# One core, state-space convolution beside windowed attention: where the next chunk's first sines stand in ScalarE's queue

## The chip, the cores and the metric

The kernel runs on one core of a Trainium2 chip. The metric is the device time of one execution in microseconds (us). The core has five engines with a queue each, in which instructions run in order: TensorE (PE in the profile), VectorE (DVE), ScalarE (ACT), GpSimd (POOL) and SyncE (SP). SyncE issues most of the transfers between the core's memory and DRAM. An engine that meets an instruction whose inputs are not there waits, and all that is queued behind the instruction waits with it.

## The reference

Two independent computations share the core; their outputs stand side by side. Part A is attention over a dilated window of 8 keys (32 heads of 20). Part B is a long convolution whose filter is a sum of 192 complex exponentials for each of 640 channels:

```python
P = jnp.exp(logdA[:, :, None] * l[None, None, :])       # (640, 192, 2048), complex
K = jnp.einsum("dn,dnl,dn->dl", Cc, P, dB).real         # the filter, 2048 long
Kf = rfft(pad(K)); Uf = rfft(pad(u))
y = irfft(Uf * Kf)[:2048] + u * Dskip
```

The output is `concatenate([attention, y])`, 2048 rows of 1280.

## The kernel before

Part B's 640 channels are worked in five chunks of 128 (`for c in range(NCH)`, L750). A position l is split into digits, so that each exponential is a product of small tables, and each chunk builds its filter in two halves (h = 0 and 1), each of two units.

- `coefficients` (L204) writes two more forms of the chunk's coefficients `cT`, and `exps_chunk` (L215) the real exponentials `R` for the whole chunk, 45 ScalarE instructions at L224. `R` has two buffers, for even and odd chunks.
- `trig_half` (L228) makes one half's sines and cosines. TensorE forms the phases in PSUM (L249, L253), and ScalarE takes the sine at L261: four instructions into `TA`, then four into `TX`. `TA` has a buffer for each half, `TX` one in all, so the next half's `TX` is written when the X products of this half have read it.
- `small_half` (L272) multiplies `R`, `cT`, `TA` and `TX` on VectorE (helper line L278, and L293) into F, G and X. Its first instruction, "P<-R,TA" in the trace, opens the half.
- Each unit makes three Y on VectorE (`y_form`, L312, four buffers), multiplies them with X on TensorE (`kgen_unit`, L327), and ScalarE copies the result into `Ksb` (L328), the chunk's filter.

The filter of chunk c is transformed in chunk c + 1. In `fwd` (L331) TensorE works in two steps (L341, L347), and ScalarE copies after each (`A` at L342, `Sg` at L348). In `products` (L352) SyncE loads the transform of the input twice from DRAM, into P1 (L358) and, with its halves exchanged, into P2 (L359, L360), and VectorE multiplies each with the filter's transform (L362). P2 lies where the first step's copy `A` lay, so its load waits until TensorE has read `A` in L347. `inverse_a` (L368) needs both products: TensorE at L378, ScalarE's copies `Z` at L379. Then comes the transform of the input for the next chunk but one (`fwd_u`, L395), with the same two steps and copies.

In a chunk above 0 the calls stand in this order: the first half's small products; the transform of the last chunk's filter; the second half's sines; unit 0; the two products and `inverse_a`; unit 1; `fwd_u`; the second half's small products; then the lines that the change touches; then units 2 and 3. After the last chunk's inverse comes attention: projection of the keys (`proj_k`, L477, and `k_halo`, L486), the chunk's last units (L327), projection of the queries (L495).

The order on an engine is not the order of the calls: a scheduler places instructions by when it takes their inputs to be ready. `issue_after(x)` queues what its block records on x's engine behind x; `keep_in_program_order` queues an instruction behind all recorded before it. PSUM has three two-bank buffers, shared by the phases, both steps of `fwd` and `inverse_a`.

Switching ScalarE between sines and exponentials takes an instruction of its own, ACT_TABLE_LOAD in the trace, put ahead of the first of the other kind.

Of the kernel before, what the change touches and what calls it, by code (L numbers as in the profile page):

```python
# [203 lines left out]
def coefficients(engine, B, c):  # L204

    co = B["cT"][:, c]
    if engine.engine == mybir.EngineType.Activation:
        engine.activation(out=co[:, :, 1], in_=co[:, :, 2], func=ACT.Copy, scale=-1.0)
        engine.copy(out=co[:, :, 3], in_=co[:, :, 0])
    else:  # L210
        engine.tensor_scalar(out=co[:, :, 1], in0=co[:, :, 2], scalar1=-1.0, scalar2=None, op0=A.mult)
        engine.tensor_copy(out=co[:, :, 3], in_=co[:, :, 0])


def exps_chunk(tc, pools, B, c):  # L215
    nc = tc.nc
    R = pools["tab"].tile([128, 48, NE_R, 4], bf16, name="R", tag=f"R{c % 2}")
    src = B["alpha"][:, c].rearrange("p u (q f) -> p (u q) f", f=4)
    nc.gpsimd.memset(R[:, :, 0:16:8, :], 1.0)
    nc.gpsimd.memset(R[:, :, 47, :], 1.0)  # L220
    for e, m in enumerate(R_MULT):
        if m == 0.0:
            continue
        last = nc.scalar.activation(out=R[:, :, e, :], in_=src, func=ACT.Exp, scale=m)  # L224
    return R, last
# [463 lines left out]
def body(tc, ctx, pools, prm, B_u, B_Dskip, Sd, Zd, UDd, A_x, A_wqkv, A_wo, out_a, out_b):  # L689
# [13 lines left out]
    R, trig = {}, {}  # L703
    with tc.tile_pool(name="prep_b", bufs=1) as pb, tc.tile_pool(name="prep_c", bufs=1) as pc, tc.tile_pool(name="prep_a", bufs=1) as pa, tc.tile_pool(name="psum_p", bufs=2, space=bass.MemoryType.PSUM) as psp:
        pools.update(prep_a=pa, prep_b=pb, prep_c=pc)
        B, fill = partB_prep(tc, dict(pools, psum=psp), prm)
# [43 lines left out]
    for c in range(NCH):  # L750
# [32 lines left out]
        with ExitStack() as order:  # L783
            if c > 0:
                order.enter_context(tc.issue_after(last.ins))
            F, G, Xs = small_half(tc, pools, B["cT"][:, c], R[c], *trig[c, 1][:2], 1)
        if c < LAST:
            if c > 0:
                with tc.issue_after(trig[c, 1][2].ins):
                    coefficients(nc.scalar, B, c + 1)  # L790
                    R[c + 1] = exps_chunk(tc, pools, B, c + 1)[0]
            trig[c + 1, 0] = trig_half(tc, pools, B, c + 1, 0)
        else:
            att.open_q0()
        with ExitStack() as order:
# [70 lines left out]
    for i0, ni, j0, nj, done in ((0, 128, 2, 3, 0), (128, 128, 2, 3, 1), (256, 128, 0, 4, None), (256, 256, 4, 1, 2), (384, 128, 0, 4, 3)):  # L866
        if done == 1:
            att.sums(1)
        for w in range(W):
# [4 lines left out]
            if (done, w) in LOADS:  # L874
                qr, c = LOADS[done, w]
# [12 lines left out]
def kernel(  # L888
# [28 lines left out]
    Zd = dpool.tile([NCH, 128, 4096], bf16, name="Zdram")  # L917
    UDd = dpool.tile([NCH, 128, 2048], bf16, name="UDdram")
    body(tc, ctx, pools, prm, B_u, B_Dskip, Sd, Zd, UDd, A_x, A_wqkv, A_wo, out_a, out_b)


# [28 lines left out]
```

## Time and profile before

| | us |
|---|---|
| median of 3 runs | 425.13 |
| lowest, highest | 423.94, 426.79 |
| the profiled execution | 420.77 |
| its span, first to last instruction | 419.0 |

The prediction quotes the profile's page and answers of the trace. A timeline row has the start (us from the span's start), the time from the first start to the last end in the row, the engine, the line, the operation, its output and input with their sizes, how many instructions the row merges, and in brackets the idle time before it and what ended that. Neighbouring instructions of one engine overlap a little, so the pace in a queue is read from start to start. A row of the chain of waits has start, length, engine or DMA, line or tile. The chunks of the loop can be told from the rows "P<-R,TA" on VectorE: chunk 2 begins with the one at 129.74, its second half at 156.80, chunk 3 at 180.62 and 207.65, chunk 4 at 230.27 and 259.49.

### The profile page before, as it was taken

The page shows a single profiled execution, that of the slowest core. Times are in us where ns is not written, and L with a number is a line of the kernel's source. Part 1 is how long each engine was busy: PE and PEld are TensorE (multiplying, and loading weights), DVE is VectorE, ACT ScalarE, POOL GpSimd, SP SyncE. Part 2 cuts the span into 40 slices and gives each one's busy share as a digit, 9 for nine tenths or more (in the row PEclk, how much of TensorE's full clock was granted, in tenths as well). Part 3 has the DMA queues.
Part 4 walks back from the last instruction along what each step waited for, and adds up shares of the span by engine and source line. Part 5 has one row for each costly group of instructions (what it writes and reads, how often), then busy time and mean ns, then how long its engine had stood idle before and what let it go on. Part 6 is the DMA issues. An engine that isn't in the chain of part 4 may idle for free.

```text
span 419.0 us, 17105 instructions
## 1 busy us (share of the span) xinstructions
PE 341.1 (81%) x7757; PEld 227.0 (54%) x7757; DVE 382.7 (91%) x381; ACT 310.5 (74%) x571; POOL 47.9 (11%) x85
## 2 busy tenths in 40 slices
PE   2375678989886887778868688999899999799996
PEld 1133463866864567455754557455555676444444
DVE  7999999999997999999999988994986899899762
ACT  3989996889999899979999492533667645754752
POOL 7540000000000000000000000170000300502110
PEclk9997598999899899989999899999999999969999
DMA  5599002164233403334029990440040292897544
GB/s 144 171 228 171 3 2 96 60 231 102 103 129 127 102 5 127 129 128 102 28 104 295 185 256 9 157 167 2 3 102 0 85 207 81 221 237 214 156 127 127
DMA packets 45129, 51.57 MB, mean 123 GB/s; under 512 B 31376, under 2 KB 38992, under 8 KB 42368
## 3 DMA queue, kind: packets, MB, share of 16 engines
q1 hardware_dynamic: 41520, 41.40, 36.7%
q0 software_dynamic: 3392, 8.95, 7.2%
q8 instruction: 61, 1.00, 1.0%
q10 hardware_dynamic: 144, 0.12, 0.1%
q14 instruction: 12, 0.10, 0.1%
HBM read 28.01 MB, written 18.35 MB: 111 GB/s over the span
## 4 chain that ended last, share of the span: by engine, by line
PE 33%; DVE 23%; ACT 19%; DMA 11%; issue 7%; SPq 6%; DVEq 0%; ACTq 0%
DVE Y L312 9%; DMA P<-Sdram 5%; ACT A L342 5%; ACT R L224 5%; PE ps_k L327 4%; PE ps_q L495 4%; PE ps_k L477 4%; PE ps_v L508 4%; PE ps_op L426 4%; DVE X L278 3%; ACT Sg L348 3%; PE ps_o L426 2%; DMA U<-in_B_u_dram 2%; DVE P L362 2%; PE ps_l L548 2%
## 5 line engine op out<-in xcount | busy, mean ns | idle before, releaser
L312 DVE TENSOR_TENSOR Y<-F,G 128x3072 bf16<-128x3072 bf16 x60 | 102.9, 1757 | 0.0
L327 PE MATMUL ps_k<-Y,X 64*32 64x64 bf16 (+1 forms) x3840 | 81.5, 237 | 20.5 <-DVE Y L312 14.5
L327 PEld LDWEIGHTS <-X 64*32 64x32 bf16 (+1 forms) x3840 | 62.2, 115 | 46.7 <-issue 32.8
L224 ACT ACTIVATE R<-LPC 128x192 bf16<-128x192 f32 x225 | 59.6, 358 | 0.1
L249 PE MATMUL ps_ph<-LPC 128*128 128x512 bf16 x100 | 32.2, 424 | 13.2 <-DMA LPC<-lo 6.2
L348 ACT CAST Sg<-ps_f 128x1024 bf16<-128x1024 f32 x40 | 37.7, 1025 | 6.1 <-PE ps_f L347 6.0
L342 ACT CAST A<-ps_f 128x1024 bf16<-128x1024 f32 x40 | 38.0, 1040 | 2.1 <-PE ps_f L341 2.0
L347 PE MATMUL ps_f<-A,T 128*128 128x128 bf16 x320 | 23.8, 235 | 16.0 <-ACT A L342 14.2
L278 DVE TENSOR_TENSOR X<-R,TX 128x1536 bf16<-128x1536 bf16 x40 | 36.5, 958 | 0.0
L261 ACT ACTIVATE TA<-ps_ph 128x1024 bf16<-128x1024 int16 (+1 forms) x40 | 30.4, 828 | 6.1 <-PE ps_ph L249 3.6
L606 DVE TENSOR_TENSOR prod<-v,atp 128x2048 bf16<-128x2048 bf16 (+2 forms) x32 | 30.8, 1018 | 2.4 <-PE ps_o L426 1.5
L347 PEld LDWEIGHTS <-T 128*128 128x128 bf16 x320 | 21.7, 106 | 17.8 <-issue 16.7
L261 ACT ACTIVATE TX<-ps_ph 128x1024 bf16<-128x1024 int16 (+1 forms) x40 | 29.6, 839 | 1.1 <-PE ps_ph L253 1.1
L537 DVE TENSOR_TENSOR prod<-qT,kT 128x1024 bf16<-128x1024 bf16 (+1 forms) x16 | 23.0, 1483 | 4.7 <-ACT qT L496 4.7
L362 DVE TENSOR_TENSOR P<-P,Sg 128x4096 bf16<-128x4096 bf16 x10 | 22.8, 2290 | 4.6 <-DMA P<-Sdram 2.6
L426 PE MATMUL ps_op<-wo,o 128*128 128x320 bf16 x160 | 26.3, 301 | 0.1
L638 ACT CAST ob<-ps_op 128x320 bf16<-128x320 f32 x28 | 12.0, 429 | 16.9 <-PE ps_op L426 15.6
L378 PE MATMUL ps_ia<-EA,P 128*128 128x128 bf16 x320 | 21.5, 220 | 2.9 <-DVE P L362 2.8
L328 ACT CAST Ksb<-ps_k 128x512 bf16<-128x512 f32 x20 | 11.7, 601 | 16.1 <-PE ps_k L327 16.0
L495 PE MATMUL ps_q<-xT,wkq 128*128 128x512 bf16 x100 | 22.6, 379 | 0.0
L477 PE MATMUL ps_k<-xT,wkq 128*128 128x512 bf16 x100 | 22.4, 379 | 0.0
L379 ACT CAST Z<-ps_ia 128x1024 bf16<-128x1024 f32 x20 | 19.4, 1014 | 3.7 <-PE ps_ia L378 3.7
(133 smaller groups left out, 601.7 us busy)
## 6 DMA issues: line engine op xcount, KB each, us to landing
Sdram<-Sg SPq DMA_DIRECT2D x5, 1024.0 KB
P<-Sdram SPq DMA_DIRECT2D x5, 1024.0 KB
P<-Sdram SPq DMA_DIRECT2D x10, 512.0 KB
Zdram<-Z SPq DMA_DIRECT2D x5, 1024.0 KB
Z<-Zdram SPq DMA_DIRECT2D x30, 128.0 KB
U<-in_B_u_dram SPq DMA_DIRECT2D x4, 640.0 KB
UDdram<-UD SPq DMA_DIRECT2D x10, 256.0 KB
out_dram<-ysb SPq DMA_DIRECT2D x32, 80.0 KB
```

Source lines behind the costliest of these rows:

```text
L224: last = nc.scalar.activation(out=R[:, :, e, :], in_=src, func=ACT.Exp, scale=m)
L249: MM(full[:, 16 * gi:16 * gi + 16], lhsT=L[b][:, 0:128], rhs=C, start=(i == 0), stop=(i == len(ops) - 1))
L261: last = nc.scalar.activation(out=dst[:, q0:q0 + nq, 0:32, :].rearrange("p q e f -> p e q f"), in_=words.rearrange("p (e q f) -> p e q f", ...
L278: TT = lambda o, a, b, op: V.tensor_tensor(out=o, in0=a, in1=b, op=op)
L312: nc.vector.tensor_tensor(out=Y[:].rearrange("p q (b a) f -> p q b a f", a=8), in0=fa, in1=gb, op=A.mult)
L327: MM(ps[32 * g:32 * g + 32, t], lhsT=X[hb, q, 2 - k, :, f], rhs=Ys[k][hb, q, :, f], start=(t == 0 and n == 0), stop=(n == 5), tile_positio ...
L342: nc.scalar.copy(out=A1[:, :, 32 * b:32 * b + 32].rearrange("p k (j g) -> p k j g", g=4), in_=ps[:].rearrange("p j k g -> p k j g"))
L347: last = MM(ps[:, kk], lhsT=C["T2"][:, 8 * b + kk, :], rhs=A1[:, 8 * b + kk, :], start=(kk % 4 == 0), stop=True, skip_group_check=True)
L348: nc.scalar.copy(out=Sg[:, :, 8 * b:8 * b + 8, :], in_=ps[:].rearrange("p k (j g) -> p j k g", g=4))
L426: self.MM = lambda *a, **k: late(self.nc.tensor.matmul(*a, **k))
L477: MM(ps[:, i], lhsT=self.wk[:, kt, 128 * ct:128 * ct + 128], rhs=self.x4[:, kt, 2 * i:2 * i + 2, 256 * hf:256 * hf + 256], start=(kt == 0) ...
L495: MM(ps[:, i], lhsT=self.wq[:, kt, 128 * ct:128 * ct + 128], rhs=self.x4[:, kt, 2 * i:2 * i + 2, 256 * hf:256 * hf + 256], start=(kt == 0) ...
```

## The change

The call that makes the sines of the next chunk's first half is moved ahead of the block with the coefficient forms and the exponentials, and the block is queued on ScalarE behind these sines (`trig_half` returns `TA`, `TX` and its last sine) instead of behind those of the current chunk's second half. This applies to c = 1, 2 and 3. In chunk 0 the block stands elsewhere, and the last chunk has no next one.

```diff
         if c < LAST:
+            trig[c + 1, 0] = trig_half(tc, pools, B, c + 1, 0)
             if c > 0:
-                with tc.issue_after(trig[c, 1][2].ins):
+                with tc.issue_after(trig[c + 1, 0][2].ins):
                     coefficients(nc.scalar, B, c + 1)
                     R[c + 1] = exps_chunk(tc, pools, B, c + 1)[0]
-            trig[c + 1, 0] = trig_half(tc, pools, B, c + 1, 0)
```

The built programs hold the same number of instructions of each kind, 11 table loads among them, and the same order on SyncE and GpSimd. ScalarE's order from the sines of chunk 1's second half on is, before: Ksb, coefficient forms, table load, 7 exponentials, Ksb, 4 exponentials, Z three times, 1 exponential, Z, A four times, 3 exponentials, Sg four times, 30 exponentials, table load, 8 sines, Ksb twice, A of the next chunk. After: Ksb twice, Z, A and Sg four times each, 8 sines, coefficient forms, table load, 45 exponentials, Ksb twice, A of the next chunk four times, Sg four times, table load, 8 sines of that chunk's second half. At the two later places the Ksb and Z stand a little differently among each other, and the exponentials that stood between the copies before are more.

The scheduler moves other work with it. On VectorE, in the first half of chunks 2 to 4, the products with the first 16 of X's 32 exponent rows come for both units first, then a Y (in chunk 4 two), then those with the other 16; and five Y stand ahead of the first L362 product and one between the two, where before three stood ahead and the other three between or behind. In chunk 4 the negation of TX (L293) comes ahead of the half's first product, too. In chunks 2 and 3 a UD product (L391) comes ahead of the second L362 instead of behind. On TensorE a few tens of kgen_unit's multiplications (37 in chunk 2, 50 in chunk 3, 13 in chunk 4) stand between the two steps of the filter's transform. In chunk 4, 15 multiplications of the inverse, 34 of kgen_unit and 48 of the inverse follow the last phase, then proj_k's 50, then all 25 of k_halo (before, 21 of these stood ahead of the inverse).

## The prediction

> **What bounds it now.** I read the page's busy times first, then the busy time by stretches of the chunks, then the timelines of VectorE and ScalarE, and last the chain of waits where the loop ends.
>
> ```profile
> span 419.0 us, 17105 instructions
> PE 341.1 (81%) x7757; PEld 227.0 (54%) x7757; DVE 382.7 (91%) x381; ACT 310.5 (74%) x571; POOL 47.9 (11%) x85
> ```
>
> ```profile
> 156.00:180.00 24.00, 18.54 (x447) 13.81 (x439) 24.00 (x23) 23.09 (x46) 0.62 (x2) 0.95 0.28 112
> ...
> 230.00:259.00 29.00, 22.16 (x683) 16.95 (x681) 25.77 (x23) 16.78 (x22) 0.15 (x1) 0.94 0.82 164
> 259.00:300.00 41.00, 39.99 (x716) 23.00 (x705) 34.74 (x34) 17.51 (x21) 9.17 (x4) 1.00 0.23 84
> ```
>
> Columns three to six are PE, PEld, DVE, ACT after the stretch and its length. In the chunks VectorE is all but full (24.00 of 24.00) and ScalarE nearly so (23.09); behind 259 TensorE is the full one (39.99 of 41.00). So an edit on ScalarE can give at most VectorE's few idle spots, and what it gives counts only if TensorE's late stretch starts earlier. VectorE's timeline holds these spots and the marks that I use:
>
> ```profile
> 101.23 2.28 DVE L362 TENSOR_TENSOR P<-P,Sg 128x4096 bf16<-128x4096 bf16 x1
> ...
> 129.74 0.96 DVE L278 TENSOR_TENSOR P<-R,TA 128x1536 bf16<-128x1536 bf16 x1 [2.33 <-ACT TA L261]
> ...
> 135.89 2.69 DVE L278 TENSOR_TENSOR X<-R,TX 128x1536 bf16<-128x1536 bf16 x3
> ...
> 146.11 2.29 DVE L362 TENSOR_TENSOR P<-P,Sg 128x4096 bf16<-128x4096 bf16 x1
> 148.31 1.75 DVE L312 TENSOR_TENSOR Y<-F,G 128x3072 bf16<-128x3072 bf16 x1
> 149.98 2.29 DVE L362 TENSOR_TENSOR P<-P,Sg 128x4096 bf16<-128x4096 bf16 x1
> ...
> 155.52 1.36 DVE L391 TENSOR_TENSOR UD<-U,Dsb 128x1024 bf16<-128x1024 bf16 x1
> 156.80 0.95 DVE L278 TENSOR_TENSOR P<-R,TA 128x1536 bf16<-128x1536 bf16 x1
> ...
> 180.62 0.96 DVE L278 TENSOR_TENSOR P<-R,TA 128x1536 bf16<-128x1536 bf16 x1
> ...
> 207.65 0.97 DVE L278 TENSOR_TENSOR P<-R,TA 128x1536 bf16<-128x1536 bf16 x1
> ...
> 230.27 0.98 DVE L278 TENSOR_TENSOR P<-R,TA 128x1536 bf16<-128x1536 bf16 x1
> ...
> 248.74 2.29 DVE L362 TENSOR_TENSOR P<-P,Sg 128x4096 bf16<-128x4096 bf16 x1 [2.00 <-ACT TA L261]
> ...
> 253.94 2.29 DVE L362 TENSOR_TENSOR P<-P,Sg 128x4096 bf16<-128x4096 bf16 x1 [1.24 <-DMA P<-Sdram]
> ```
>
> There are three idle spots, and only the first, 2.33 us ahead of chunk 2, waits for the sines that the change moves. Chunks 3 and 4 start without a wait. In chunk 4 the waits of 2.00 and 1.24 are for loads (the sine named at 248.74 can't be it, since that product reads none).
>
> **ScalarE's queue, step by step.** These rows give the pace of each kind:
>
> ```profile
> 100.06 0.42 ACT L208 ACTIVATE cT<-cT 128x192 bf16<-128x192 bf16 x1
> ...
> 100.73 1.28 ACT L224 ACT_TABLE_LOAD   x1
> ...
> 114.05 3.76 ACT L348 CAST Sg<-ps_f 128x1024 bf16<-128x1024 f32 x4 [0.33 <-PE ps_f L347]
> 117.67 7.73 ACT L224 ACTIVATE R<-LPC 128x192 bf16<-128x192 f32 x30
> 125.42 1.28 ACT L261 ACT_TABLE_LOAD   x1
> 126.71 2.92 ACT L261 ACTIVATE TA<-ps_ph 128x1024 bf16<-128x1024 int16 x4
> ...
> 132.26 1.16 ACT L328 CAST Ksb<-ps_k 128x512 bf16<-128x512 f32 x2
> 133.20 3.88 ACT L342 CAST A<-ps_f 128x1024 bf16<-128x1024 f32 x4
> ```
>
> From start to start: coefficient forms 100.73 - 100.06 = 0.67, table load 126.71 - 125.42 = 1.29, one exponential (125.42 - 117.67) / 30 = 0.258, eight sines 132.26 - 126.71 = 5.55, two Ksb 0.94.
>
> Nothing is removed or added; the gain must come from order. Before, the chunk's first product needs two table loads, all 45 exponentials (15 of them slipped in between the copies) and four sines. After, it needs eight sines, the forms, one load and the 7 exponentials of the first eight rows; the others run beside VectorE. The price is that the slots among the copies, once used by 15 exponentials, the forms and a load (15 x 0.258 + 0.67 + 1.29 = 5.8 us), fall empty, because TensorE feeds the copies there no faster:
>
> ```profile
> 103.57 3.84 PE L378 MATMUL ps_ia<-EA,P 128*128 128x128 bf16 x61 [0.60 <-DVE P L362]
> 107.33 4.04 PE L341 MATMUL ps_f<-BD,U 128*64 128x128 bf16 x64
> 113.00 3.42 PE L347 MATMUL ps_f<-A,T 128*128 128x128 bf16 x32 [1.63 <-ACT A L342]
> ```
>
> The inverse starts as the second product ends (101.23 + 2.28 = 103.51), the next transform right behind it until 111.37, and the second step at 113.00. Sg ends at 117.81, 14.3 after the product. Without exponentials in between, the last copy of A could start some 0.5 us earlier, at 111.4; so Sg ends 13.8 after the product (bounds 13.3 and 14.3). From there: exponentials begin at 13.8 + 5.55 + 0.67 + 1.29 = 21.3 behind the second product; 7 are done at 23.1, 14 (for G) at 24.9, 30 (first X products) at 29.0, all 45 at 32.9.
>
> At one place a rule speaks against the new order. The row has the next activation 1.29 after the load starts. The Trainium skill, page "ScalarE: Activation LUTs", section "What ACT_TABLE_LOAD costs", puts a switch at about 1.28 us for the load and 1.38 for a drain. By that the load, which the new order keeps on the way to a chunk's first product, would hold each of the three starts up to 1.38 more, about 2.7 us in all after the margins found below, and the sum would come out some 1.2 us slower than before; the trace shows the 1.28 and no drain.
>
> **Chunk 2.** VectorE is free at 129.74 - 2.33 = 127.41, the seven exponentials are there at 103.51 + 23.1 = 126.6, G's at 128.4 against 128.3. P starts at about 127.5, 2.2 us earlier. The first X product comes 135.89 - 129.74 = 6.2 later, at 133.7, and the third, behind two X (2.69 / 3 = 0.9 each) and a Y (149.98 - 148.31 = 1.67), at 137.1; their rows are there at 132.5 and 136.4, so they don't wait.
>
> The exponentials that were early are now late for ScalarE's next work: they end at 136.4, so the copies A of the filter's transform start at 137.3 instead of 133.20, and the P2 load, which waits for them, moves with it. This takes the row of the load's issue and its flight from the chain of waits:
>
> ```profile
> 140.51 0.45 SPq L359 DMA_DIRECT2D P<-Sdram  x1
> ```
>
> ```profile
> 141.01 6.34 DMA P<-Sdram
> ```
>
> ```profile
> 191.56 6.45 DMA P<-Sdram
> ```
>
> ```profile
> 244.39 9.43 DMA P<-Sdram
> ```
>
> From A's start to the issue it was 140.51 - 133.20 = 7.3; so it is issued at 144.7 and has landed at 144.7 + 0.5 + 6.34 = 151.5. VectorE comes to the second product later than before, as two Y and a UD now stand ahead: 127.5 + (146.11 - 129.74) + 2 x 1.67 + (149.98 - 146.11) + 1.28 = 152.4. So the load is covered by 0.9 us. The product ends at 154.6, and, with those Y and UD done already, the second half starts there instead of at 156.80: 2.2 us are kept.
>
> **Chunks 3 and 4.** From the second half's start to the next chunk's P VectorE takes 180.62 - 156.80 = 23.8 against ScalarE's 23.1: no wait, P at 178.4. All 45 exponentials are there at 187.5, the load at 187.5 + 0.9 + 7.3 + 0.5 + 6.4 = 202.6, and VectorE comes to it 24.9 after P, at 203.3 (margin 0.7). The second half starts at 205.5 instead of 207.65. To chunk 4 it is 230.27 - 207.65 = 22.6 of VectorE with, in the new order, a TX negation (0.47) moved ahead of P, so P falls at 228.6, even with ScalarE. In chunk 4 the exponentials end at 238.4, A starts at 239.4, P2 is issued at 246.7 and lands at 253.6, later than VectorE's 251.7. Here the load ends last, as it did before at 253.94, and the gain shrinks. I take 6.45 for it: its 9.43 of before flew beside the P1 load, which waited behind the transposes of x:
>
> ```profile
> 225.82 16.42 SPq L436 DMA_TRANSPOSE xT<-in_A_x_dram  x4
> 242.34 0.52 SPq L358 DMA_DIRECT2D P<-Sdram  x1
> ```
>
> The transposes stand behind the store of a UD in SyncE's queue and start 2 us earlier with it, so P1 goes out at about 240.3, and it is done before P2 starts. The second product ends at 255.8.
>
> ```profile
> 255.10 0.69 PE L486 MATMUL ps_kh<-xT,wkq 128*128 128x42 bf16 x21
> ...
> 262.71 10.95 PE L477 MATMUL ps_k<-xT,wkq 128*128 128x512 bf16 x50
> ```
>
> Behind it TensorE has 63 multiplications of the inverse (3.84 by the row of 61 above) and 34 of a unit (0.8), with no Y left to wait for, where before it waited for two: proj_k starts at about 260.5 instead of 262.71, 2.2 earlier. Of these 0.7 go to the 21 multiplications of k_halo that filled a gap before and now stand behind proj_k. **Sum: 1.5 us earlier**, handed on whole through the stretch that TensorE fills. Against the profiled execution that is 420.8 - 1.5 = 419.3; that execution is 4.4 below the median of the three runs, and the same 1.5 off the median gives 423.6.
>
> **Rivals.** *The load is on time in chunk 4 too* (lands by 251.7): then proj_k starts 1.9 earlier still, 3.4 in all, 421.7. For it speaks that TensorE's second step in chunk 4 may run closer behind A than in chunk 2, against it the transposes beside it (the DMA share is 0.82 in 230 to 259).
>
> *The sines are held by TensorE.* The phases stand between a unit's multiplications in TensorE's queue, and one gap of this kind is in the trace:
>
> ```profile
> 177.56 0.60 ACT L261 ACTIVATE TA<-ps_ph 128x512 bf16<-128x512 int16 x1 [0.89 <-PE ps_ph L253]
> ...
> 180.93 0.60 ACT L261 ACTIVATE TX<-ps_ph 128x512 bf16<-128x512 int16 x1 [0.36 <-PE ps_ph L253]
> ```
>
> With 0.89 + 0.36 = 1.25 in each chunk, less the margins 0.8, 0.7 and 0, the three starts lose 2.3, and the end is 0.8 later than before, 425.9. Against it, the first chunk's and the later sines of the trace ran without a gap.
>
> *Slower: the P2 load takes the wait's place.* It is now issued 4 us later in each chunk and covered by only 0.9 and 0.7. If it takes 9.43 instead of 6.4, the second product waits 2.2, 2.3 and 3.0, and each wait delays the inverse, the copies, the sines and the exponentials behind it, so they add: 7.5 - 1.5 = 6.0 slower, 431.1. It decides from a flight of about 7.3 us on. Against it: both undisturbed flights took 6.4.
>
> That the change does nothing is excluded by the order of ScalarE's queue; that its effect is lost is the second rival.
>
> **Numbers.** Chances: my forecast 0.50, on time in chunk 4 0.15, held sines 0.20, late load 0.15. A measurement of this kernel can tell about 1% (4.3 us) from no change; its three runs alone spread over 2.9. My forecast's own range is 421.5 to 425.5. The whole range is from 421.7 less half that spread, 420.0, to past the held sines, 428.0; the late load's upper part is left out. Faster by over 1% only by the first rival with scatter, 0.10; slower the late load, 0.15; within 1% 0.75.
>
> **What would show it.** Right: no wait for a sine ahead of chunk 2's P, chunk 3's and 4's P at about 178 and 229, ScalarE empty for some 5 us among the copies, 45 exponentials in one run, and L477 starting 2 us earlier. Wrong: waits on "P<-R,TA" or G for R in chunks 3 and 4, a wait for P<-Sdram ahead of the second L362 in chunks 2 or 3, gaps between sines for ps_ph, or a late stretch of another length behind L477.

## The result, and the profile after

| | before | after |
|---|---|---|
| median of 6 runs, us | 424.53 | 428.71 |
| lowest to highest, us | 419.50 to 427.67 | 425.18 to 430.08 |
| the profiled execution, us | 420.77 | 429.62 |

The changed kernel takes 1.0125 of the time before, with a 95% interval of 1.0078 to 1.0171: some 1.2% slower. The forecast was 0.4% faster. Ratios here and below leave out executions more than 1.5% above the fastest of their kernel, and three of the profiles below are of such executions (the new order in chunks 1 and 2 alone, half of the units' multiplications in the old order, fewer exponentials in the new one).

The page of the changed kernel shows that the engines' busy times hardly grew, but for TensorE's (by 4.1 us, of which 4.0 lie in the run's last stretch, shown below; VectorE and ScalarE by 0.8 each):

```profile
span 427.8 us, 17099 instructions
PE 345.2 (81%) x7757; PEld 227.2 (53%) x7757; DVE 383.5 (90%) x381; ACT 311.3 (73%) x571; POOL 41.2 (10%) x85
```

So up to that last stretch waits are what is new. Among the page's groups, the Y on VectorE show it; the last field is the idle time ahead of them and what ended it. First the group before, then after:

```profile
L312 DVE TENSOR_TENSOR Y<-F,G 128x3072 bf16<-128x3072 bf16 x60 | 102.9, 1757 | 0.0
```

```profile
L312 DVE TENSOR_TENSOR Y<-F,G 128x3072 bf16<-128x3072 bf16 x60 | 103.4, 1764 | 4.9 <-PE ps_k L327 4.9
```

Before, no Y ever waited. Now VectorE, the engine that is all but full, waits 4.9 us for TensorE to read an earlier Y and free its buffer, 4.3 of them ahead of the projection of the keys (L477). VectorE's timeline after has the places:

```profile
103.10 0.99 DVE L278 TENSOR_TENSOR P<-R,TA 128x1536 bf16<-128x1536 bf16 x1
...
126.95 0.99 DVE L278 TENSOR_TENSOR P<-R,TA 128x1536 bf16<-128x1536 bf16 x1
128.46 0.96 DVE L278 TENSOR_TENSOR G<-R,TA 128x1536 bf16<-128x1536 bf16 x1 [0.52 <-ACT R L224]
...
154.63 0.96 DVE L278 TENSOR_TENSOR P<-R,TA 128x1536 bf16<-128x1536 bf16 x1
...
174.51 1.76 DVE L312 TENSOR_TENSOR Y<-F,G 128x3072 bf16<-128x3072 bf16 x1 [0.52 <-PE ps_k L327]
176.71 1.76 DVE L312 TENSOR_TENSOR Y<-F,G 128x3072 bf16<-128x3072 bf16 x1 [0.45 <-PE ps_k L327]
...
180.74 0.96 DVE L278 TENSOR_TENSOR P<-R,TA 128x1536 bf16<-128x1536 bf16 x1 [1.01 <-ACT R L224]
...
207.84 0.94 DVE L278 TENSOR_TENSOR P<-R,TA 128x1536 bf16<-128x1536 bf16 x1
...
231.44 0.96 DVE L278 TENSOR_TENSOR P<-R,TA 128x1536 bf16<-128x1536 bf16 x1 [0.46 <-ACT R L224]
...
252.61 1.76 DVE L312 TENSOR_TENSOR Y<-F,G 128x3072 bf16<-128x3072 bf16 x1 [3.31 <-PE ps_k L327]
...
258.15 2.28 DVE L362 TENSOR_TENSOR P<-P,Sg 128x4096 bf16<-128x4096 bf16 x1
```

The wait of 2.33 us for a sine ahead of chunk 2 is gone, and the second half of chunk 2 opens at 154.63 instead of 156.80. By chunk 3 (180.74 against 180.62) the lead is lost: two Y wait for TensorE, then the chunk's first product for its exponentials. In chunk 4 another Y waits 3.31 us.

TensorE's timeline after tells why it is late (a merged row's length runs from its first start to its last end):

```profile
136.81 1.07 PE L341 MATMUL ps_f<-BD,Ksb 128*64 128x128 bf16 x16 [6.43 <-ACT Ksb L328]
...
140.92 2.67 PE L347 MATMUL ps_f<-A,T 128*128 128x128 bf16 x24
...
153.98 2.30 PE L327 MATMUL ps_k<-Y,X 64*32 64x64 bf16 x122
156.80 0.88 PE L327 MATMUL ps_k<-Y,X 64*32 64x64 bf16 x38 [0.52 <-issue]
157.62 1.01 PE L378 MATMUL ps_ia<-EA,P 128*128 128x128 bf16 x15
...
257.55 2.83 PE L327 MATMUL ps_k<-Y,X 64*32 64x64 bf16 x150
261.70 0.29 PE L327 MATMUL ps_k<-Y,X 64*32 64x64 bf16 x8 [1.32 <-issue]
261.92 1.01 PE L378 MATMUL ps_ia<-EA,P 128*128 128x128 bf16 x15
...
266.33 10.96 PE L477 MATMUL ps_k<-xT,wkq 128*128 128x512 bf16 x50
...
281.22 2.12 PE L495 MATMUL ps_q<-xT,wkq 128*128 128x512 bf16 x9
```

In the middle of the filter's transform TensorE stands still for 6.43 us, until ScalarE copies Ksb (the same wait is 6.44 in chunk 3 and 3.42 in chunk 4). What it could not do then it does later, together with the multiplications of the second unit, and the inverse runs in earnest only from 157.62, 3.0 us behind the product that it was waiting for. ScalarE's timeline after shows the other side:

```profile
123.46 1.28 ACT L224 ACT_TABLE_LOAD   x1
124.76 11.53 ACT L224 ACTIVATE R<-LPC 128x192 bf16<-128x192 f32 x45
136.17 1.07 ACT L328 CAST Ksb<-ps_k 128x512 bf16<-128x512 f32 x2
137.11 3.75 ACT L342 CAST A<-ps_f 128x1024 bf16<-128x1024 f32 x4
...
154.09 0.60 ACT L261 ACTIVATE TX<-ps_ph 128x512 bf16<-128x512 int16 x1 [1.47 <-PE ps_ph L253]
...
158.71 1.01 ACT L379 CAST Z<-ps_ia 128x1024 bf16<-128x1024 f32 x1 [3.54 <-PE ps_ia L378]
...
167.32 3.76 ACT L348 CAST Sg<-ps_f 128x1024 bf16<-128x1024 f32 x4 [0.69 <-PE ps_f L347]
```

All 45 exponentials come in one run, the Ksb copies start behind them at 136.17 (before: 132.26), and later ScalarE in turn waits for TensorE, 1.47 us ahead of a sine and 3.54 ahead of the first Z. The chain of waits that ended last goes the same way where the loop ends: in chunk 4 it runs from the exponentials (until 240.99) over Ksb and A to TensorE's second step at 245.62, and stays with TensorE until past 261. Busy time by the halves of chunk 2 (the stretch, its length, then PE, PEld, DVE, ACT, POOL, and behind them the granted clock) makes the shift plain, before and after:

```profile
129.70:156.80 27.10, 21.03 (x557) 15.61 (x549) 27.07 (x23) 25.93 (x51) 0.00 (x0) 0.94 0.27 76
156.80:180.60 23.80, 18.34 (x412) 13.52 (x403) 23.80 (x23) 22.85 (x43) 0.62 (x2) 0.94 0.28 113
```

```profile
127.00:154.60 27.60, 17.85 (x440) 12.22 (x432) 27.08 (x24) 24.77 (x57) 0.00 (x0) 0.80 0.34 97
154.60:180.70 26.10, 22.96 (x650) 17.90 (x641) 24.16 (x23) 21.70 (x34) 0.62 (x2) 0.95 0.24 95
```

TensorE does 117 multiplications fewer in the first half and 238 more in the second, which takes 26.10 us instead of 23.80.

To compare executions I use one distance D: from the P<-R,TA that opens chunk 1's second half (103.43 before, 103.10 after) to the start of L477. It is 262.71 - 103.43 = 159.3 before and 266.33 - 103.10 = 163.2 after. These 3.9 us of the chunk loop are about the 4.2 between the medians. The two profiled executions lie 8.9 apart; the other 5.0 stand in their ends, where the same number of multiplications met a slower clock after (first row before, second after):

```profile
372.00:419.00 47.00, 42.46 (x816) 21.52 (x816) 32.89 (x36) 24.22 (x51) 6.56 (x12) 0.96 0.57 162
```

```profile
375.00:427.00 52.00, 46.42 (x816) 22.35 (x815) 34.41 (x37) 24.58 (x51) 6.55 (x12) 0.87 0.54 152
```

From the start of L477 to the end of the span it is 156.3 us before and 161.5 after. In the kernels of the next section, whose work there is the same, it doesn't go with the order of the sines: 155.7 in one with the new order (the second of "VectorE's order"), 160.8 in one with the old (the first of "Copies earlier"). So I count it neither for nor against the change.

### The profile page after: what moved, and what is told of

It is laid out like the page before. It is cut to its first block, busy times and chain, and to the rows that moved or that the text cites. A ratio compares the mean times of both kernels' runs of the same rounds, so it can differ in the third digit from the quotient of the medians.

```text
span 427.8 us, 17099 instructions
## 1 busy us (share of the span) xinstructions
PE 345.2 (81%) x7757; PEld 227.2 (53%) x7757; DVE 383.5 (90%) x381; ACT 311.3 (73%) x571; POOL 41.2 (10%) x85
## 4 chain that ended last, share of the span: by engine, by line
PE 39%; ACT 23%; DVE 22%; DMA 6%; issue 5%; SPq 3%; DVEq 0%; ACTq 0%
DVE Y L312 9%; ACT R L224 8%; PE ps_op L426 6%; PE ps_k L327 5%; PE ps_q L495 4%; ACT A L342 4%; DVE X L278 4%; PE ps_k L477 4%; PE ps_v L508 4%; PE ps_o L426 3%; PE ps_f L347 2%; DMA U<-in_B_u_dram 2%; ACT TX L261 2%; PE ps_l L548 2%; PE ps_ph L249 2%
## 5 line engine op out<-in xcount | busy, mean ns | idle before, releaser
L327 PE MATMUL ps_k<-Y,X 64*32 64x64 bf16 (+1 forms) x3840 | 84.6, 237 | 22.7 <-issue 10.6
L224 ACT ACTIVATE R<-LPC 128x192 bf16<-128x192 f32 x225 | 58.2, 359 | 0.1
L347 PE MATMUL ps_f<-A,T 128*128 128x128 bf16 x320 | 25.0, 241 | 9.7 <-ACT A L342 8.2
L426 PE MATMUL ps_op<-wo,o 128*128 128x320 bf16 x160 | 29.9, 328 | 1.5 <-issue 1.3
L341 PE MATMUL ps_f<-BD,Ksb 128*64 128x128 bf16 x320 | 14.2, 244 | 19.4 <-ACT Ksb L328 16.3
L347 PEld LDWEIGHTS <-T 128*128 128x128 bf16 x320 | 22.5, 109 | 11.4 <-issue 9.9
L362 DVE TENSOR_TENSOR P<-P,Sg 128x4096 bf16<-128x4096 bf16 x10 | 22.9, 2292 | 1.4 <-DMA P<-Sdram 1.4
L341 PEld LDWEIGHTS <-Ksb 128*64 128x64 bf16 x320 | 11.6, 124 | 21.9 <-ACT Ksb L328 16.8
L495 PE MATMUL ps_q<-xT,wkq 128*128 128x512 bf16 x100 | 22.6, 379 | 0.0
L477 PE MATMUL ps_k<-xT,wkq 128*128 128x512 bf16 x100 | 22.4, 379 | 0.0
```

The lines of the kernel that those rows point to most:

```text
L327: MM(ps[32 * g:32 * g + 32, t], lhsT=X[hb, q, 2 - k, :, f], rhs=Ys[k][hb, q, :, f], start=(t == 0 and n == 0), stop=(n == 5), tile_positio ...
L347: last = MM(ps[:, kk], lhsT=C["T2"][:, 8 * b + kk, :], rhs=A1[:, 8 * b + kk, :], start=(kk % 4 == 0), stop=True, skip_group_check=True)
L426: self.MM = lambda *a, **k: late(self.nc.tensor.matmul(*a, **k))
L477: MM(ps[:, i], lhsT=self.wk[:, kt, 128 * ct:128 * ct + 128], rhs=self.x4[:, kt, 2 * i:2 * i + 2, 256 * hf:256 * hf + 256], start=(kt == 0) ...
L495: MM(ps[:, i], lhsT=self.wq[:, kt, 128 * ct:128 * ct + 128], rhs=self.x4[:, kt, 2 * i:2 * i + 2, 256 * hf:256 * hf + 256], start=(kt == 0) ...
```

## The experiments

Two explanations stood against each other. T: TensorE is the one that is late; the transform's copies queue behind 45 exponentials, TensorE idles, and then has the transform, the phases and two units at once. S: it is ScalarE's own queue that is too long between the sines and the next chunk. The other letters are explained in the expectations themselves. One profile's D is not exact: two profiles of the changed kernel differ by 1.1, and one idle spot of TensorE by up to 1.7 us between kernels (last section), so I read differences of D below 2 us only together with the waits and the ratio. Ratios are to the kernel before, with 95% intervals.

**Which chunk pays.** The new order in chunks 1 and 2 alone, and in chunk 3 alone (with `(3,)` for `(1, 2)`):

```diff
+            if c in (1, 2):
+                trig[c + 1, 0] = trig_half(tc, pools, B, c + 1, 0)
             if c > 0:
-                with tc.issue_after(trig[c + 1, 0][2].ins):
+                with tc.issue_after(trig[(c + 1, 0) if c in (1, 2) else (c, 1)][2].ins):
...
+            if c not in (1, 2):
+                trig[c + 1, 0] = trig_half(tc, pools, B, c + 1, 0)
```

> The new order in chunks 1 and 2, the old one in chunk 3. Theory A (the loss falls due in the chunk after the changed one, where the filter's transform stands behind the 45 exponentials, and is paid in full only where VectorE's head start of 2.5 us is already used up): chunk 4's first half runs as before, proj_k starts within 1 us of 262.7, time within 2 us of the kernel before. Rival B (each changed chunk costs the same): two thirds of the loss, 2.5 to 3.5 us slower than before, proj_k at about 265. Rival C (the loss is only TensorE's slow stretches at the end of the run, which have nothing to do with the edit): proj_k anywhere, time as that of the changed kernel on average.

> The new order in chunk 3 only, the old one in chunks 1 and 2. Theory A: chunk 4 starts no earlier than before (VectorE doesn't wait there for sines), its transform is 4 us late as in the changed kernel, and the whole loss is paid: proj_k at 265.5 to 267, 3 to 5 us slower than before. Rival B: a third of the loss, 1 to 2 us slower, proj_k at about 264. Rival C: no difference from before in proj_k.

Chunks 1 and 2: ratio 1.004 (0.9986 to 1.0094), D 163.6. Chunk 3: 1.0142 (1.0057 to 1.0226), D 164.4. The first ratio is smaller than its D suggests (4.3 us would be 1.0%, just above the interval's end). None of the three expectations holds by D: chunk 4 doesn't run as before (A), two changed chunks don't cost two thirds (B), and the start of L477 does move (C). The loss isn't confined to the changed order in chunk 3: with that order taken back, chunk 4 has to wait for its sines (VectorE's timeline of the first of the two kernels):

```profile
238.61 0.96 DVE L278 TENSOR_TENSOR P<-R,TA 128x1536 bf16<-128x1536 bf16 x1 [6.42 <-ACT TA L261]
```

ScalarE starts the coefficient forms for chunk 4 at 208.90 there, where the kernel before starts them at 198.48, and the old order then needs all exponentials before the sines. One chunk's new order leaves a debt to the next. In the kernel with chunk 3 alone, 3.0 us were lost before the changed lines, in a wait for a load in chunk 3's first half; from the opening of chunk 3's second half to L477 it takes 268.31 - 211.62 = 56.7, against 55.1 before and 58.5 after, so the order in chunk 3 costs some 1.6 by itself, which one profile can hardly tell from nothing. Whether the wait for the load came back in its other executions no profile shows, so its ratio isn't read further.

**Fewer exponentials in a row.** The forms and 15 exponentials stand where they stood before the change, then come the next sines, then the other 30, for two more table loads in each chunk (`exps_chunk` takes the rows to make, from and up to; the lines are shown against the changed kernel):

```diff
-            trig[c + 1, 0] = trig_half(tc, pools, B, c + 1, 0)
             if c > 0:
-                with tc.issue_after(trig[c + 1, 0][2].ins):
+                with tc.issue_after(trig[c, 1][2].ins):
                     coefficients(nc.scalar, B, c + 1)
-                    R[c + 1] = exps_chunk(tc, pools, B, c + 1)[0]
+                    R[c + 1], last = exps_chunk(tc, pools, B, c + 1, None, 0, 17)
+                with tc.issue_after(last.ins):
+                    trig[c + 1, 0] = trig_half(tc, pools, B, c + 1, 0)
+                with tc.issue_after(trig[c + 1, 0][2].ins):
+                    exps_chunk(tc, pools, B, c + 1, R[c + 1], 17)
+            else:
+                trig[c + 1, 0] = trig_half(tc, pools, B, c + 1, 0)
```

> In chunks 1 to 3 the coefficient forms and the first 15 exponentials stand behind the current half's sines, as before, to fill the slots among the copies; then come the next half's sines, then the other 30 exponentials. Two table loads more per chunk (2.6 us of ScalarE). Theory A (what costs is how late ScalarE ends its exponentials, since the next transform is queued behind them; what gains is that the first product needs few of them): P of chunk 2 still at about 127, exponentials end at about 133.7 against 136.2, Ksb and A 2.5 us earlier than in the changed kernel, proj_k at 263 to 264.5, time 1.5 to 3 us under the changed kernel's. Rival D (ScalarE is so full that the two loads more eat it): time as the changed kernel's or above.

Ratio 1.0035 (0.9981 to 1.0089), D 159.8. ScalarE's timeline of this kernel (its line numbers are two higher here):

```profile
125.84 7.71 ACT L226 ACTIVATE R<-LPC 128x192 bf16<-128x192 f32 x30
133.45 1.04 ACT L330 CAST Ksb<-ps_k 128x512 bf16<-128x512 f32 x2
```

The copies start 2.7 us earlier than in the changed kernel, and D falls by 3.4 although ScalarE has more to do. So what counts is how many exponentials stand ahead of the copies, and not how much ScalarE does in all; between T and S this doesn't decide, since the queue behind the sines became shorter too. It is not faster than the kernel before.

**The clock.** TensorE runs at half clock after its idle time (2.67 us for 24 multiplications of L347, 0.80 granted in that half chunk). Multiplications whose result nobody reads fill the idle spot, first 24 in the transforms of chunk 1's and 2's filters and 12 in that of chunk 3's, then 30 and 15 with 6 more ahead of the second step:

```diff
+        if b == 2 and extra:
+            with tc.issue_after(first.ins):
+                for _ in range(extra):
+                    MM(ps[:, 0:4].rearrange("p j k g -> p (j k g)"), lhsT=C["T2"][:, 0, :], rhs=C["T2"][:, 0:4, :].rearrange("p a n -> p (a n)"), start=True, stop=True, skip_group_check=True)
```

> The changed kernel with idle multiplications (24, 24 and 12 of 128x128 by 512) in TensorE's queue ahead of the third group of the filter's transform in chunks 2, 3 and 4, written where that group's own first multiplication then starts anew: they fill the 6.4 us in which TensorE waits for Ksb behind the exponentials. Theory A1 (half of the loss is the clock that falls in that wait: after it the second step's 24 multiplications took 2.67 us against 1.50): the granted clock stays at 1.00 through 130 to 145, the second step is about 1.2 us quicker, proj_k starts 1 to 3 us earlier than in the changed kernel (263.5 to 265.5). Rival A2 (the clock is a by-product, the loss is only that the transform is queued late and bunches with the unit's multiplications): proj_k stays within 0.7 us of 266.3.

> As warm_tensor, with 30, 30 and 15 idle multiplications ahead of the third group and 6 more ahead of the second step, so that TensorE has no wait of over 1 us from 129 to 145. If the fall of the clock is a large part, it stays at 1.00 through 145, the second step's 24 multiplications take 1.5 us instead of 2.7, and proj_k starts 1 to 3 us earlier than in the changed kernel. If bunching alone is the loss, proj_k stays within 0.7 us of the changed kernel or comes later by what the idle multiplications overshoot.

The first fell short: the granted clock still fell, to 0.84 in 136 to 138 and 0.50 behind that, and it tells nothing beyond its ratio, 1.0254 (1.0167 to 1.034), and D, 166.6. The second kept the clock at 1.00 from 126 to 152. TensorE's timeline of it (L355 is the second step, L386 the inverse):

```profile
140.91 1.50 PE L355 MATMUL ps_f<-A,T 128*128 128x128 bf16 x24
...
157.52 1.01 PE L386 MATMUL ps_ia<-EA,P 128*128 128x128 bf16 x15
```

The second step takes 1.50 instead of 2.67, and the inverse still starts at 157.52, 0.1 earlier than in the changed kernel. In chunk 2, then, the slow clock is a companion of the loss and not its cause. Over the whole loop the added multiplications are themselves a load on TensorE: ratio 1.017 (1.0093 to 1.0247), D 166.4.

**Less work for TensorE.** Half of each unit's multiplications is left out, in both orders:

```diff
-    runs = [(k, tail) for k in range(3) for tail in ((k + u) % 2, 1 - (k + u) % 2)]
+    runs = [(k, 0) for k in range(3)]
```

> The kernel before without half of kgen_unit's multiplications (the second run of 64 for each of the three Y is left out, 192 of 384 for a pair of units, so the last 64 of its 192 terms a position are missing from the filter). A base for the next run: VectorE's work is the same, TensorE has some 3.7 us less in each half chunk. Both theories: 0 to 6 us quicker than the kernel before, mostly behind 262, where TensorE is full.

> The changed kernel with the same half of kgen_unit's multiplications left out. Theory T (the new order loses because the filter's transform, the phases and the units' multiplications now fall together on TensorE, which then holds the fifth Y and the inverse): with TensorE lightened VectorE no longer waits for ps_k, the inverse starts with the second product, and the new order is no slower than its base of the run before, down to the 1.5 us quicker that I had forecast. Theory S (the new order loses on ScalarE alone, through the slots left empty among the copies, 5.8 us a chunk, and whatever is queued behind the exponentials): it stays 3 to 5 us slower than its base.

The row of L477 in TensorE's timeline, old order and new:

```profile
264.23 10.95 PE L477 MATMUL ps_k<-xT,wkq 128*128 128x512 bf16 x50
```

```profile
260.67 10.95 PE L477 MATMUL ps_k<-xT,wkq 128*128 128x512 bf16 x50
```

D is 160.4 with the old order and 157.6 with the new; the ratios to the full kernel before are 0.9945 (0.9853 to 1.0038) and 0.9879 (0.9779 to 0.9979). The two ratios' intervals overlap, but the sign in the chunk loop turns round: the new order, 3.9 us later with the full units, is 2.8 us earlier with half of them. The size is not firm, and larger than T expected (up to 1.5): this base waits 4.23 us for its sines ahead of chunk 2, where the full kernel before waited 2.33. But 157.6 is also under the 159.3 of that full kernel, and the place of the loss shows it without the base. In the new order TensorE's wait for Ksb in chunk 2 is even longer here:

```profile
137.82 1.06 PE L341 MATMUL ps_f<-BD,Ksb 128*64 128x128 bf16 x16 [11.37 <-ACT Ksb L328]
```

Still the inverse runs from 155.80, as its product ends (153.46 + 2.29 = 155.75), no Y waits in chunk 2 (in chunk 4 two wait 1.2 us together), and the chunk's second half takes 179.50 - 155.66 = 23.8, as in the kernel before, instead of 26.1. ScalarE has the same work to do as with full units, and S expected the loss to stay, so S is refuted, and T holds: the late copies cost when TensorE has no room to catch up. The clock is no rival either, since the second step takes 2.67 here too.

**Copies earlier, new order kept.** The last 15 exponentials are left out (their rows of R are set to 1), again in both orders:

```diff
-        if m == 0.0:
+        if m == 0.0 or e >= 32:
```

> The kernel before without the last 15 exponentials of each chunk (the rows 32 to 46 of R are set to 1, so the second half of X's factors is not the real one). A base for the next run: ScalarE has 3.9 us less in each chunk. Both theories: the wait of 2.33 ahead of chunk 2 goes, 1 to 3 us quicker than the kernel before.

> The changed kernel with the same 15 exponentials left out: its filter's transform is queued behind 30 exponentials instead of 45, 3.9 us earlier, at the place it had before the change. Theory S: the loss against the base of the run before goes for the most part, to 0 to 1.5 us, and VectorE doesn't wait for ps_k. Theory T: TensorE's load is the same, only earlier by 3.9 us, so a part of the loss goes with the bunching, 1 to 3 us stay.

Ratios 1.0047 (0.9962 to 1.0132) and 1.0028 (0.9971 to 1.0085); D 157.4 and 158.3 (chunk 1 began its second half 4.8 us late in both, so these two compare only with each other). With the transform's copies 15 x 0.258 = 3.9 us earlier the new order costs 0.9 in D, within what two profiles can tell from nothing, and nothing in the time, though the base no longer waits for its sines and the new order has nothing to gain. The 0.9 lies where S expected it (0 to 1.5) and just under T's 1 to 3, so this pair alone doesn't part the two. And VectorE's order fell back here too, to three Y ahead of the products, so it left one more rival, which the last two runs take up.

**The changed kernel again.**

> The changed kernel once more, unaltered, for a second profile. If the loss up to proj_k belongs to the order of the work, VectorE's waits for ps_k come again in chunks 2 and 4 and proj_k starts 163 (within 1 us) after the second half of chunk 1 begins, against 159.3 before; time 0.7 to 1.7% over the kernel before. If it was the chance of one execution, proj_k comes at 158 to 161. The two stretches of half clock in the last 45 us of the first profile may stand elsewhere or be fewer.

Ratio 1.0163 (1.0098 to 1.0228), D 164.3. Its TensorE and VectorE timelines repeat the pattern to 0.2 us:

```profile
137.38 1.06 PE L341 MATMUL ps_f<-BD,Ksb 128*64 128x128 bf16 x16 [6.44 <-ACT Ksb L328]
```

```profile
254.47 1.76 DVE L312 TENSOR_TENSOR Y<-F,G 128x3072 bf16<-128x3072 bf16 x1 [3.50 <-PE ps_k L327]
```

**Two tries at a remedy.** Ksb's copies ahead of the last 15 exponentials in the changed kernel:

```diff
-                    R[c + 1] = exps_chunk(tc, pools, B, c + 1)[0]
+                    R[c + 1] = exps_chunk(tc, pools, B, c + 1, None, 0, 32)[0]
...
-        unit(c, 1, 1, F, G, Xs[1], q_first if c == LAST else lambda: None)
+        done = unit(c, 1, 1, F, G, Xs[1], q_first if c == LAST else lambda: None)
+        if 0 < c < LAST:
+            with tc.issue_after(done.ins):
+                exps_chunk(tc, pools, B, c + 1, R[c + 1], 32)
```

> The changed kernel with the last 15 exponentials of each chunk queued behind the two Ksb copies instead of ahead of them: TensorE gets the last two groups of the filter's transform 3.7 us earlier, while the copies A, behind all exponentials, stay where they were. If the wait of TensorE in itself (and the clock that falls in it) is the loss, proj_k starts 1 to 3 us earlier than in the changed kernel. If it is the lateness of A, and with it of the second step, the phases and P2, nothing moves by more than 0.7 us, and X may wait 0.2 to 0.5 us for its last rows.

Ratio 1.0329 (1.0268 to 1.039), D 170.0, the slowest of all. ScalarE's timeline:

```profile
131.63 1.04 ACT L330 CAST Ksb<-ps_k 128x512 bf16<-128x512 f32 x2
132.57 3.90 ACT L226 ACTIVATE R<-LPC 128x192 bf16<-128x192 f32 x15
136.38 3.71 ACT L344 CAST A<-ps_f 128x1024 bf16<-128x1024 f32 x4
```

Ksb came 4.5 us earlier, but the other 15 exponentials then stood ahead of the A copies, which hardly moved (137.11 in the changed kernel); TensorE waits twice, 2.51 and 4.54 us, instead of once. Why it is so much worse than the changed kernel, and not even with it, I could not settle.

And the split order of above in chunk 1 alone, in the kernel before (`c > 0` becomes `c == 1`):

> The split order (forms and 15 exponentials, the next half's sines, 30 exponentials) in chunk 1 alone, the old order in chunks 2 and 3. Only chunk 2 waited for sines before; there the split takes the wait of 2.3 us away and ends the exponentials 1.2 us after the place they had, instead of 3.9. By what the runs have shown so far chunk 3's P then starts 2.3 us earlier without a wait (sines at 177.1, VectorE free at 178), the transform in chunk 4 is on time, proj_k starts 1.5 to 2.5 us earlier than before the change, and the time is 0.3 to 0.6% under the kernel before. If ScalarE can't make up the two table loads, P of chunk 3 waits 1 us or more and the gain is under 1 us.

Ratio 1.0034 (0.9992 to 1.0076), D 160.2. Chunk 2 gains as in the split kernel, and chunk 3 pays it back, as VectorE's timeline shows:

```profile
181.65 0.96 DVE L280 TENSOR_TENSOR P<-R,TA 128x1536 bf16<-128x1536 bf16 x1 [3.67 <-ACT TA L263]
```

No order that I ran beats the kernel before.

**VectorE's order.** The scheduler had also put five Y ahead of the products, not three. The first kernel puts five Y ahead of them in the kernel before; the second, with `range(0)` and `more(1)` in the places of `range(2)` and the first `more(3)`, has in its trace four Y ahead of the products and two behind both in chunk 2 of the changed kernel (`products` calls its last argument between the two):

```diff
-            P1, P2, last = products(tc, pools, Sk[c - 1], Sd[c - 1], fp, True)
+            Ys = [y_form(tc, pools, F, G, 1, k) for k in range(2)]
+            more = lambda n: Ys.extend(y_form(tc, pools, F, G, 1, k) for k in range(len(Ys), n))
+            P1, P2, last = products(tc, pools, Sk[c - 1], Sd[c - 1], fp, True, lambda: more(3))
+            with tc.issue_after(last.ins):
+                more(3)
```

> The kernel before with one thing of the changed kernel: VectorE's order of the Y. The two Y of the second unit are made ahead of the first L362 product and one between the two products, as in the changed kernel; ScalarE's sines and exponentials keep their order. Number: the start of L477 less the start of the P<-R,TA that opens the second half of chunk 1 (159.3 in the kernel before, 163.2 and 164.3 in the changed one). Theory T (TensorE gets the transform's copies late, behind the 45 exponentials, and then has too much at once): the order on VectorE alone does little, 159 to 161, waits of Y for ps_k below 0.5 us in all, TensorE's wait ahead of the third group of L341 stays below 1 us. Theory O (the products stand behind the Y, and the scheduler's new order of VectorE is the loss): 162 to 164, with waits of Y for ps_k of some 3 us or more in chunk 4.

> The changed kernel with VectorE's order mended: four Y (not five) stand ahead of the first L362 product, then both products, then the last two Y. ScalarE's order of sines and exponentials is that of the changed kernel. Theory T: TensorE's wait of about 6.4 us ahead of the third group of L341 stays; the Y no longer wait 3.3 us in chunk 4, but the products wait for the P2 load instead (it lands at about 151.5 and 256.5), so L477 less the opening of chunk 1's second half is 162.5 to 165, and the time is within 0.5% of the changed kernel's. Theory O: with the products no longer behind a fifth Y the loss goes, 159 to 161, and the time is that of the kernel before or 0.3% below.

Five Y in the kernel before: ratio 1.0065 (1.0 to 1.0131), D 161.4. The order alone makes Y wait, on VectorE's timeline:

```profile
201.16 1.76 DVE L312 TENSOR_TENSOR Y<-F,G 128x3072 bf16<-128x3072 bf16 x1 [2.21 <-PE ps_k L327]
...
251.70 1.76 DVE L312 TENSOR_TENSOR Y<-F,G 128x3072 bf16<-128x3072 bf16 x1 [0.81 <-PE ps_k L327]
```

That is more than T expected and less than O: the order has a part in it, about half by this profile (161.4 - 159.3 = 2.1 of 3.9) and by the ratio, and some of that may stem from an idle spot of TensorE of 2.42 us in chunk 3 that the kernel before has with 1.00. Mending the order in the changed kernel brings nothing back: ratio 1.0136 (1.007 to 1.0202), D 163.7, as T expected, and TensorE's wait for Ksb in chunk 2 stays (6.16 us). No Y waits there, and the second products wait for P2 instead, in chunks 2 and 4 (and 2.12 us in chunk 3; 3.25 in chunk 1, which lies ahead of D's mark and is in the ratio alone):

```profile
153.34 2.29 DVE L362 TENSOR_TENSOR P<-P,Sg 128x4096 bf16<-128x4096 bf16 x1 [2.00 <-DMA P<-Sdram]
...
261.44 2.29 DVE L362 TENSOR_TENSOR P<-P,Sg 128x4096 bf16<-128x4096 bf16 x1 [3.99 <-DMA P<-Sdram]
```

So the late transform costs about the same either way. It makes the P2 load late; with few Y ahead, the product waits for it, and with five ahead they cover the load, and a Y waits for TensorE. How the loss divides between the late copies and the order of the Y stays open.

## Why the prediction was wrong

*The sine's wait goes, and chunk 2's second half opens at 154.6.* Right: P at 126.95 (forecast 127.5), A at 137.11 (137.3), the P2 load covered, the second half at 154.63. G waited 0.52 for its exponential, where the forecast had 0.1. The exponentials come in one run of 45. By this point the kernel is 2.2 us ahead, less the 0.3 by which the two profiles' marks differ.

*Sg ends 13.8 after the second product.* This is the step that failed. The sum started TensorE's inverse as the product ends, because it did before. It held in chunk 1, where the exponentials begin at 124.76 (forecast 124.8). In chunk 2 Sg ends at 171.1, 16.4 behind the opening of the second half; in chunk 3 at 221.84, 14.0 behind it. The forecast had seen the A copies move by 4 us and followed that delay to the P2 load alone. It did not follow it to TensorE, which waits for the same copies, and whose unit multiplications then fall behind the phases and into the inverse's place. The half-unit pair shows that this is what decides, and the kernel with the mended VectorE order that the loss isn't won back there.

*Chunk 3 to chunk 4, and the rest of the sum.* From each of the forecast's marks to the next it lost as follows: chunk 2's second half took 180.74 - 154.63 = 26.1 instead of 23.8 (2.3 lost: two Y, and the exponentials late behind the late Sg); chunk 3's first half 27.1 as forecast, its second 23.6 instead of 23.1 (0.5); chunk 4's first half until the second product ends 260.43 - 231.44 = 29.0 instead of 27.2 (1.8, the Y's 3.31 in place of the load's wait); from there to L477 5.9 instead of 4.7 (1.2). Together 5.8, which is 266.33 - 260.5. The load in chunk 4, which the forecast held to be the gate, was never waited for, though it went out later than forecast (249.48 instead of 246.7).

*"With no Y left to wait for".* Here a second step failed, the 4.7 us from the second product's end to L477. The forecast had the inverse start as the product ends, with 97 multiplications from there to L477. In the trace TensorE comes to 158 multiplications of a unit only at 257.55, behind the last phase (the list of the new order under "The change" leaves them out), and they end at 262.0 with an idle spot among them; the inverse starts 1.5 us behind the product's end at 258.15 + 2.28 = 260.43.

*k_halo behind proj_k.* Right in kind, smaller in size: from L477 to L495 it takes 281.22 - 266.33 = 14.9, against 277.19 - 262.71 = 14.5 in the kernel before, 0.4 instead of 0.7.

*The rivals.* The first one, the load on time in chunk 4, came so far as nothing waited for that load, but only because the Y ahead of it waited longer. The second one, the sines held by TensorE, named the right engine and put it at 0.8 us slower. But its own gaps hardly came: of the moved sines only those for chunk 2 met any, 0.23 and 0.40 us. The 1.47 stands ahead of a sine of the second half, and the 3.54 ahead of the first Z; it had left out both. Nor did its counter-argument hold that the trace has one gap of this kind: sines at 69.09, 70.50 and 96.34 of the kernel before waited 0.79, 0.39 and 0.25 for their phases. The slower rival, the load in the wait's place, didn't show in the changed kernel but is what the mended VectorE order brings out, with 2.0 to 4.0 us a chunk. The drain that the Trainium skill ("ScalarE: Activation LUTs", "What ACT_TABLE_LOAD costs") adds to a table load is not seen after either: the next exponential starts 124.76 - 123.46 = 1.30 after the load's start. So the slower time isn't that page's.

The median of 428.71 lies 0.7 above the range; the range's upper end had been built from gaps of the old order.

## What to carry to other kernels

When a step is moved in one engine's queue, follow the delay of what now stands behind it to every engine that reads it, not only to the transfer or the wait that is nearest; a full queue of cheap work ahead of four copies can starve the engine that those copies feed. Check whether an engine that looked idle "on average" had its idle time where the new order needs it: here TensorE was busy 18.3 of the 23.8 us of chunk 2's second half before, and the new order brought 4.6 more into it. And an order that interleaves many short instructions between copies may look untidy in the trace, and cost table loads, and still be what lets two engines run side by side.

## What the hardware showed beyond that

TensorE's clock: behind a wait of 6.43 us the groups of 16 multiplications of L341 take 1.07 us, and the 24 of L347 2.67, where 24 take 1.50 when the idle spot is filled. The Trainium skill ("TensorE: Matmul & The Clock Gate", "What's actually happening") has the clock at either half or full, falling after an idle window of about 3.4 us. On half and full these rows agree with it (16 multiplications of L341 take 0.64 at full clock). On when it falls they differ: in the changed kernel the granted clock is 1.00 until 133.0 and 0.65 in 133.0 to 133.5, so it falls some 2.8 us after TensorE's last multiplication (129.30 + 1.08 = 130.38), and in the first kernel with idle multiplications it falls behind 137 with no gap above 1.47 us in the 9 us ahead. At the kernel's end the same 816 multiplications are granted 0.96 in the profile before and 0.87 in that after, which is worth 4 us of busy time, as much as the change itself: the length of one profiled execution doesn't measure a change of 1%.

TensorE also has idle spots that the profile puts down to nothing but issue. Ahead of 45 multiplications in chunk 3, in the kernel before, in that with the new order in chunk 3 alone (which is not reached yet at that point) and in that with five Y:

```profile
185.11 1.47 PE L341 MATMUL ps_f<-BD,Ksb 128*64 128x128 bf16 x45 [1.00 <-issue]
```

```profile
188.80 1.49 PE L341 MATMUL ps_f<-BD,Ksb 128*64 128x128 bf16 x45 [2.67 <-issue]
```

```profile
188.27 1.47 PE L341 MATMUL ps_f<-BD,Ksb 128*64 128x128 bf16 x45 [2.42 <-issue]
```

In the two profiles of the changed kernel the spot at this place is 0.94 and 1.52 us. What ends them stays open.
